# Two interleaved layers on one core: four weight halves kept in layer B's buffer, first loads by whole units, x first, and the first step's last projection by halves

## The chip, the cores and the metric

The kernel runs on one core of one Trainium2 chip. The metric is device time in microseconds (us), median of several runs. The profiled execution is one more run; the profile gives its span, from the first to the last instruction, and its own time is 1.7 us longer.

## The reference

Two kinds of layer follow each other twice: A, B, A, B, each with a layer norm before and a residual sum behind it.

```
def _A_ref(x, mem0, Wq, Wk, Wv, Wo, seg_len):      # Dm = 640, 32 heads of 192, 8 memory rows, segments of 32
    for s in range(n_seg):                         # S = 2048, so 64 segments
        h = concatenate([mem, xs], axis=1)         # 8 + 32 rows
        q, k, v = h @ Wq, h @ Wk, h @ Wv
        p = softmax(where(mask, q @ k.T * scale, -1e9))
        o = (p @ v) @ Wo
        mem = o[:, :M]                             # goes into the next segment
        outs.append(o[:, M:])

def _B_ref(x, wqkv, wo):                           # 32 heads of 20, window of 8 keys, two apart
    q, k, v = x @ wqkv
    return softmax(q . k[pos - 2 * (0..7)]) . v @ wo

x = x + A(layernorm(x));  x = x + B(layernorm(x))
x = x + A(layernorm(x));  x = x + B(layernorm(x))
```

Layer A is sequential over its 64 segments, since each segment's first 8 output rows are the memory of the next. Both A layers use the same weights, and so do both B layers. All tensors are bf16. Layer A's four weights have 640 x 6144 elements each, 31.5 MB together, more than the core's on-chip memory holds.

## The kernel before

**Steps and lanes.** `run` calls `step(t)` for t from 0 to 66. Lane 0 holds the first A, B pair at segment t, lane 1 the second pair at segment t - 2, so a two-lane step multiplies 2 x 40 = 80 columns by each weight. Steps 0 and 1 have lane 0 alone, steps 64 and 65 lane 1 alone (40 columns), and step 66 is `b_alone`, a last block of layer B. Layer B in step t works on the block that layer A finished in step t - 1; so step 0 has no layer B, and step 1 is the first that needs its weights.

**A step.** The heads of layer A are taken four at a time, in 8 quads. For each quad `i`: keys (`a_k`), queries (`a_q`), the product with the values of the quad before (`a_pv`), values (`a_v`, in one-lane steps by `a_v_rows` for all quads but 2 and 3), and scores (`a_s`). From quad 5 on the output projection of quad `i - 5` (`a_o`) comes between; the last ones follow behind quad 7, and `a_o(7)` is the last, after which `mem_out` copies the memory into the next step's input `hT`. Layer B is woven in: its queries and keys (`b_q`, `b_k`) behind the values of quad 1, its values (`b_v`) at quad 2, its output (`b_wo`) at quad 6.

**Weights.** Each of the 32 units (kind k, q, v or o, quad 0 to 7) is cut into two halves of 128 rows x 1920 elements (480 KB, 3,840 bytes in each row). Of the 64 halves 41 stay on chip from the first step on (`resident_halves`); 23 are streamed again in every step through a ring of 4 buffers (`w_ring`). The first four of the streamed ones are, in order of use, one half each of k0, v0, k1 and v1; the next are both halves of k2, one of v2, one of k3, one of q3. `self.loads` is the list of all loads in order: the 64 halves of the first step, the 23 of the second with the four parts of layer B's weights put between them, then 23 for each later step. `prefetch` takes from its front as long as the first entry is resident, a part of layer B, or a ring buffer is free; `used` gives a ring buffer back. First loads take a half in one transfer, later ones in two pieces of 960 elements (1,920 bytes in each row).

**Queues.** All these loads are issued by SP, in the order of the list, and each waits on SP until its buffer is free and until the transfer that used the same one of eight DMA semaphores before it has landed. The loads of x for later steps go by ScalarE's queue at quad 1 and take their turn in the same round of semaphores. The order of work on each engine is written out by hand (`manual_schedule`).

**Layer B's buffers** `wqkv_sb` (three parts of 5 x 640 elements in each partition) and `wo_sb` (one such part) are filled once, in step 1, and stay empty before that.

**The beginning.** `build_consts` clears the constants and buffers on VectorE, the two input buffers `xin` among them. `prologue` issues the load of x (which waits for that clearing), then that of the memory `m0T`, then the weights; the scheduler places the instructions of this part. In step 0 `warm(16)` puts 16 matmuls without use ahead of each of the last output projections.

Of the kernel before, what the change touches and what calls it, by code (L numbers as in the profile page):

```python
# [19 lines left out]
NC = 5  # L20
# [58 lines left out]
class Kernel:  # L79
    def __init__(self, ctx, tc, A_x, A_mem0, A_Wq, A_Wk, A_Wv, A_Wo, B_wqkv, B_wo, out):  # L80
# [33 lines left out]
    def build_consts(self):  # L114
# [20 lines left out]

        self.hT = pers("hT", [P, NC * NT + 88], 1)[0]
# [5 lines left out]
        self.xin = pers("xin", [P, 2, NC, SEG], 2)  # L142
# [8 lines left out]
        self.wqkv = cp.tile([P, 3, NC, D], BF16, name="wqkv_sb")  # L151
        self.wo = cp.tile([P, NC, D], BF16, name="wo_sb")

    def load_b_weights(self, part):

        w = self.wqkv[:, part] if part < 3 else self.wo[:]
# [53 lines left out]
    def prefetch(self):  # L210

        while self.loads and (self.loads[0] in self.resident or self.loads[0][0] == "b" or self.ring_free):
            key = self.loads.pop(0)
            if key[0] == "b":
                self.load_b_weights(key[1])
                continue
            if key in self.resident:
                t_ = self.wres.tile([P, HALF], BF16, name="w_%s%d%d" % key)
            else:
                t_ = self.wring.tile([P, HALF], BF16, name="w_ring")  # L220
                self.ring_free -= 1
            kind, i, h = key
            piece = HALF if self.n_loaded < N_HALVES else PIECE
            self.n_loaded += 1
            for c0 in range(0, HALF, piece):
                self.nc.sync.dma_start(out=t_[:, c0:c0 + piece], in_=self.wsrc[kind][i, h, :, c0:c0 + piece])
            self.units[key] = t_[:].rearrange("p (a b) -> p a b", a=3 if kind == "o" else NC)

    def used(self, kind, i, halves=(0, 1)):

        for h in halves:
            if (kind, i, h) not in self.resident:
                del self.units[kind, i, h]
                self.ring_free += 1
        self.prefetch()
# [136 lines left out]
    def a_o(self, i, part=slice(None), done=True):  # L372
# [5 lines left out]
        order = [(m, c) for m in (0, 2, 3, 5, 1, 4) for c in range(NC)]  # L378
        if i == NQUAD - 1:
            order = [(m, c) for m in (0, 2) for c in range(3)] + [(m, c) for c in range(3) for m in (3, 5, 1, 4)] + [(m, c) for c in range(3, NC) for m in (0, 2, 3, 5, 1, 4)]  # L380
        for m, c in order[part]:
            acc, k = self.acc_of(c)
            nc.tensor.matmul(self.cols(acc[:, k]), lhsT=w[m // 3][:, m % 3, P * c:P * (c + 1)], rhs=self.cols(ot[:, m]),  # L383
                             start=(i == 0 and m == 0 and k == 0), stop=(i == NQUAD - 1 and m == 4), skip_group_check=True)
# [255 lines left out]
    def prologue(self):  # L640
        nc = self.nc
        self.x1, self.ots, self.qxs, self.ebs = {}, {}, {}, {}
        self.x_load(0)
# [132 lines left out]
    def step(self, t):  # L776
# [75 lines left out]
        if t == 0:  # L852
            self.warm(16)
        if nt < T:
            self.ln1_apply(nt)
        self.a_o(7)
# [36 lines left out]
def _lay_out(name, a):  # L893
# [44 lines left out]
```

## Time and profile before

| | |
|---|---|
| runs, median | 3140.94 us (3138.48, 3140.94, 3144.32) |
| profiled execution | 3137.52 us |
| its span | 3135.8 us |
| TensorE busy, matmuls | 3079.3 us, 98% of the span, 83,424 matmuls |
| VectorE, ScalarE, GpSimd busy | 76%, 59%, 18% |
| mean granted clock of TensorE | 0.991 |
| moved by DMA | 786.99 MB, mean 251 GB/s |
| loads of ring buffers, 240 KB each | some 3.8 to 4.1 us from issue to landing |

In a row of a timeline stand the start, the length, the engine, the line, the operation with its operands, the count, and in brackets the idle time before it with what ended it. In the sums over stretches of time each engine's busy time is followed by its count of instructions, and at the end stand the granted clock, the share in which the 16 DMA engines were busy (it can pass 1, as packets overlap) and the rate in GB/s. "issue" is time in which an engine waited for nothing that the profile shows. Of a group of matmuls the length includes the last one's way through the array, about 0.2 us.

### The profile page before, as it was taken

Reading aid. Unit: us, or ns where it says so; the run is one execution under the profiler, and the core shown is the slowest. Engines: PE = TensorE matmul, PEld = TensorE weight load, DVE = VectorE, ACT = ScalarE, POOL = GpSimd, SP = SyncE. Lnnn points to the kernel's source line nnn. Section 1 sums busy time; section 2 is a strip of 40 time slices with the busy share of each in tenths; the row PEclk is TensorE's granted clock in tenths of the full one; section 3 lists DMA queues with packets and bytes.
Section 4 is the critical chain, followed back from the end, with each engine's and each line's share of the span. In section 5 each row is a group of like instructions: output and inputs, shape, how many; then the busy total and the mean of one; then the engine's idle time right before and its main releaser. Section 6 shows DMA issues by size and latency. Waiting matters only on the chain.

```text
span 3135.8 us, 187153 instructions
## 1 busy us (share of the span) xinstructions
PE 3079.3 (98%) x83424; PEld 3031.1 (97%) x83424; DVE 2369.9 (76%) x6012; ACT 1849.2 (59%) x5616; POOL 551.5 (18%) x1025
## 2 busy tenths in 40 slices
PE   6899999999999999999999999999999999999998
PEld 4899999999999999999999999999999999999997
DVE  3677777777777777777777777777777777777775
ACT  2456656656656656656656656656655655655654
POOL 2111111111111111111111111111111111121121
PEclk7999999999999999999999999999999999999999
DMA  9888877777878778887878878877777777877776
GB/s 387 302 249 245 250 243 247 246 245 243 248 246 247 246 246 248 248 247 246 249 244 250 249 246 248 250 241 247 249 245 248 249 242 249 249 246 248 249 250 212
DMA packets 455706, 786.99 MB, mean 251 GB/s; under 512 B 58864, under 2 KB 445680, under 8 KB 454896
## 3 DMA queue, kind: packets, MB, share of 16 engines
q1 hardware_dynamic: 441216, 769.80, 77.8%
q8 instruction: 652, 10.68, 1.4%
q10 hardware_dynamic: 13680, 5.21, 0.7%
q14 instruction: 158, 1.29, 0.1%
HBM read 772.19 MB, written 2.62 MB: 247 GB/s over the span
## 4 chain that ended last, share of the span: by engine, by line
PE 96%; DMA 3%; issue 1%; DVE 0%; ACT 0%; SPq 0%; ACTq 0%
PE ps_acc L383 18%; PE ps_k L266 18%; PE ps_q L266 18%; PE ps_v L266 17%; PE ps_vt L320 5%; PE ps_o L353 5%; PE ps_s L332 2%; PE ps_s L333 2%; PE ps_bs L549 2%; PE ps_bk L497 2%; PE ps_by L608 1%; PE ps_bv L497 1%; PE ps_bq L497 1%; DMA w_q<-in_A_Wq_dram 1%; PE ps_vr L300 1%; PE ps_bo L575 1%
## 5 line engine op out<-in xcount | busy, mean ns | idle before, releaser
L357 ACT ACTIVATE R<-ps_o 64x160 f32<-64x160 f32 (+1 forms) x2112 | 622.1, 295 | 339.3 <-PE ps_o L353 121.3
L266 PEld LDWEIGHTS <-w_ring 128*128 128x128 bf16 x16530 | 679.8, 100 | 23.2 <-issue 7.3
L266 PE MATMUL ps_q<-hT,w_q 128*128 128x80 bf16 (+1 forms) x12870 | 541.8, 201 | 4.0 <-DMA w_q<-in_A_Wq_dram 3.4
L534 POOL TENSOR_TENSOR QX<-QB,hmask 128x448 bf16<-128x448 bf16 (+2 forms) x325 | 304.7, 946 | 1346.1 <-ACT QB L512 1028.2
L266 PEld LDWEIGHTS <-w_q 128*128 128x128 bf16 x12870 | 494.2, 100 | 5.3 <-DMA w_q<-in_A_Wq_dram 4.4
L383 PE MATMUL ps_acc<-OT,w_o 128*128 128x80 bf16 (+1 forms) x9900 | 458.9, 201 | 4.2 <-issue 2.2
L278 ACT CAST KF<-ps_k 128x320 bf16<-128x320 f32 (+1 forms) x528 | 218.9, 415 | 411.8 <-PE ps_k L266 401.5
L311 DVE CAST vT<-ps_v 128x480 bf16<-128x480 f32 (+1 forms) x504 | 329.1, 653 | 163.7 <-PE ps_v L266 145.9
L285 DVE CAST QT<-ps_q 128x480 bf16<-128x480 f32 (+1 forms) x528 | 337.4, 639 | 120.9 <-PE ps_q L266 117.9
L266 PE MATMUL ps_v<-hT,w_v 128*128 128x80 bf16 (+1 forms) x9480 | 423.1, 201 | 2.0 <-DMA w_v<-in_A_Wv_dram 1.1
L383 PEld LDWEIGHTS <-w_o 128*128 128x128 bf16 x9900 | 393.2, 100 | 5.0 <-issue 2.3
L266 PE MATMUL ps_k<-hT,w_ring 128*128 128x80 bf16 (+1 forms) x7920 | 374.3, 201 | 6.6 <-DMA w_ring<-in_A_Wk_dram 2.5
L266 PE MATMUL ps_k<-hT,w_k 128*128 128x80 bf16 (+1 forms) x7920 | 374.0, 201 | 4.3 <-issue 3.3
L266 PEld LDWEIGHTS <-w_v 128*128 128x128 bf16 x9480 | 371.4, 100 | 1.5 <-DMA w_v<-in_A_Wv_dram 1.4
L335 ACT ACTIVATE E<-ps_s 80x320 bf16<-80x320 f32 (+1 forms) x528 | 221.1, 419 | 240.0 <-PE ps_s L333 240.0
L367 DVE TENSOR_TENSOR OT<-ps_o,R 128x320 bf16<-128x320 f32 (+1 forms) x528 | 253.9, 481 | 138.4 <-ACT R L359 117.2
L266 PEld LDWEIGHTS <-w_k 128*128 128x128 bf16 x7920 | 321.8, 100 | 5.0 <-issue 3.5
L322 DVE COPY Vt<-ps_vt 80x768 bf16<-80x768 bf16 x504 | 279.1, 554 | 58.3 <-PE ps_vt L320 46.6
L383 PE MATMUL ps_acc<-OT,w_ring 128*128 128x80 bf16 (+1 forms) x5940 | 307.8, 201 | 2.2 <-DMA w_ring<-in_A_Wo_dram 2.2
L266 PE MATMUL ps_v<-hT,w_ring 128*128 128x80 bf16 (+1 forms) x5640 | 264.6, 201 | 0.7 <-DMA w_ring<-in_A_Wv_dram 0.6
L341 DVE TENSOR_TENSOR E<-E,maskA 80x320 bf16<-80x320 bf16 (+1 forms) x528 | 206.3, 391 | 65.3 <-ACT E L335 54.9
L320 PE MATMUL ps_vt<-ident,vT 128*128 128x128 bf16 x3024 | 253.4, 220 | 0.9 <-DVE On L590 0.9
(146 smaller groups left out, 4914.3 us busy)
## 6 DMA issues: line engine op xcount, KB each, us to landing
w_ring<-in_A_Wk_dram SPq DMA_DIRECT2D x1040, 240.0 KB, 3.8
w_ring<-in_A_Wv_dram SPq DMA_DIRECT2D x780, 240.0 KB, 4.1
w_ring<-in_A_Wo_dram SPq DMA_DIRECT2D x780, 240.0 KB, 3.8
w_ring<-in_A_Wq_dram SPq DMA_DIRECT2D x390, 240.0 KB, 3.9
w_q<-in_A_Wq_dram SPq DMA_DIRECT2D x13, 480.0 KB, 8.8
w_v<-in_A_Wv_dram SPq DMA_DIRECT2D x10, 480.0 KB, 9.6
w_o<-in_A_Wo_dram SPq DMA_DIRECT2D x10, 480.0 KB, 9.6
w_ring<-in_A_Wk_dram SPq DMA_DIRECT2D x8, 480.0 KB, 7.7
```

Of the source, the lines that this page charges most:

```text
L266: nc.tensor.matmul(ps[:, NT * n + self.c0:NT * n + self.c1], lhsT=w[n // 3][:, c, P * (n % 3):P * (n % 3 + 1)], rhs=hT[:, NT * c + self.c0 ...
L278: nc.scalar.copy(out=kf, in_=pv[:, :, 0:3:2, :])
L285: self.nc.vector.tensor_copy(out=self.cols(qt[:]), in_=self.cols(ps[:, 0:6 * NT].rearrange("p (a n) -> p a n", a=6)))
L311: nc.vector.tensor_copy(out=self.cols(self.vT[:, 0:6 * NT].rearrange("p (a n) -> p a n", a=6)), in_=self.cols(ps[:, 0:6 * NT].rearrange("p ...
L320: nc.tensor.transpose(out=ps[:, n, :], in_=self.vT[:, NT * n:NT * n + P], identity=self.ident[:])
L322: nc.vector.tensor_copy(out=vt[0:NT, :].rearrange("p (a b c) -> p a b c", a=2, b=2)[:, :, :, 0:DH], in_=ps[0:NT].rearrange("p (a b) c -> p ...
L335: nc.scalar.activation(out=self.cols(e[0:NT]), in_=self.cols(sv[0:NT]), func=ACT.Exp, scale=float(DH) ** -0.5)
L341: nc.vector.tensor_tensor(out=self.cols(e[0:NT]), in0=self.cols(e[0:NT]), in1=self.cols(self.maskA[0:NT, :]).unsqueeze(1).to_broadcast([NT ...
L357: nc.scalar.activation(out=self.cols(r[r0:r0 + 64, :, j]), in_=self.cols(src), func=ACT.Ln)
L367: nc.vector.tensor_tensor(out=oc[:, :, 0:3:2], in0=ov[:, :, 0:4:3], in1=r, op=ALU.mult)
L383: nc.tensor.matmul(self.cols(acc[:, k]), lhsT=w[m // 3][:, m % 3, P * c:P * (c + 1)], rhs=self.cols(ot[:, m]), start=(i == 0 and m == 0 an ...
L534: self.nc.gpsimd.tensor_tensor(out=qx[:, 0:nh, self.on], in0=self.qb[:, c, self.on].unsqueeze(1).to_broadcast([P, nh, n]), in1=self.hmask[ ...
```

## The change

It has four parts.

- **Four halves kept.** `wqkv_sb` and `wo_sb` become one tile, `wb_sb`, of the same size. In the first step the first four streamed halves are loaded into it, at elements 0, 6400, 8320 and 10240 of each partition, and stay for their second use in step 1. The second step's list holds streamed halves 4 to 7, then the four parts of layer B's weights together, then the other streamed halves. A part of layer B's weights is loaded when the halves that lie in its place have been used twice; `prefetch` returns until then, so what follows it in the list waits too. From step 2 on all 23 halves go through the ring as before.
- **Whole units by rows of 7,680 bytes.** The two halves of a unit now lie side by side in memory. Where both are resident, the first step loads them with one transfer into one tile, except the last output projection's. This makes 15 transfers out of 30. Streamed halves are still loaded in pieces of 1,920 bytes, now from rows 7,680 bytes apart.
- **x first.** The load of x is issued in `build_consts`, ahead of the clearing; the half of `xin` that it fills is not cleared any more. m0 and the weights follow.
- **The last projection by halves.** In step 0 `a_o(7)` runs as 15 matmuls on its first half of the weights and 15 on its second, with 8 warming matmuls ahead of the first and 16 ahead of the second. The second 15 finish the columns of the first accumulator before those of the other.

```diff
-        second = list(streamed)
-        for at, part in ((4, 0), (5, 1), (8, 2), (18, 3)):
-            second.insert(at, ("b", part, 0))
+        self.kept = streamed[:4]
+        self.kept_uses = {u: 0 for u in self.kept}
+        second = streamed[4:8] + [("b", part, 0) for part in range(4)] + streamed[8:]
...
+        self.xin = pers("xin", [P, 2, NC, SEG], 2, zero=False)
+        self.x_load(0)
...
-        self.xin = pers("xin", [P, 2, NC, SEG], 2)
+        nc.vector.memset(self.xin[0][:, 1], 0.0)
+        nc.vector.memset(self.xin[1][:], 0.0)
...
+        self.wb = cp.tile([P, 4 * NC * D], BF16, name="wb_sb")
+        wb = self.wb[:].rearrange("p (a c n) -> p a c n", a=4, c=NC)
+        self.wqkv, self.wo = wb[:, 0:3], wb[:, 3]
+        self.kept_at = dict(zip(self.kept, (0, 2 * NC * D, 2 * NC * D + HALF, 2 * NC * D + 2 * HALF)))
+
+    def under(self, part):
+
+        lo, hi = part * NC * D, (part + 1) * NC * D
+        return [u for u in self.kept if self.kept_at[u] < hi and self.kept_at[u] + HALF > lo]
...
+            if kind == "b":
+                if any(self.kept_uses[u] < 2 for u in self.under(i)):
+                    return
+                self.loads.pop(0)
+                self.load_b_weights(i)
                 continue
+            if first and key in self.kept:
+                at = self.kept_at[key]
+                t_ = self.wb[:, at:at + HALF]
+            elif key in self.resident:
+                n += h == 0 and (kind, i, 1) in self.resident and (kind, i) != ("o", NQUAD - 1)
+                t_ = self.wres.tile([P, n * HALF], BF16, name="w_%s%d%d" % key)
...
+            piece = n * HALF if first else PIECE
+            self.n_loaded += n
+            for c0 in range(0, n * HALF, piece):
+                self.nc.sync.dma_start(out=t_[:, c0:c0 + piece], in_=self.wsrc[kind][i, :, h * HALF + c0:h * HALF + c0 + piece])
...
+        if t == 0:
+            order = [(m, c) for m in (0, 2, 1) for c in range(NC)] + [(m, c) for cs in ((0, 1, 2), (3, 4)) for m in (3, 5, 4) for c in cs]
+            self.warm(8)
+            self.a_o(7, slice(0, 3 * NC), False, order)
+            self.warm(16)
+            self.a_o(7, slice(3 * NC, None), True, order)
+        else:
+            self.a_o(7)
...
-        return a.reshape(NC, P, NQUAD, 2, QE // 2).transpose(2, 3, 1, 0, 4).reshape(NQUAD, 2, P, HALF)
+        return a.reshape(NC, P, NQUAD, 2, QE // 2).transpose(2, 1, 3, 0, 4).reshape(NQUAD, P, 2 * HALF)
...
-        return a.reshape(NQUAD, 2, 3, P, D).transpose(0, 1, 3, 2, 4).reshape(NQUAD, 2, P, HALF)
+        return a.reshape(NQUAD, 2, 3, P, D).transpose(0, 3, 1, 2, 4).reshape(NQUAD, P, 2 * HALF)
```

More of the change, by code (lines that the diff above doesn't have):

```diff
@@ L220, in prefetch @@
                 t_ = self.wring.tile([P, HALF], BF16, name="w_ring")
                 self.ring_free -= 1
[L222 to L227, printed above, removed]
+            else:
+                return
@@ L231, in used @@
         for h in halves:
-            if (kind, i, h) not in self.resident:
-                del self.units[kind, i, h]
-                self.ring_free += 1
+            u = (kind, i, h)
+            if u in self.resident:
+                continue
+            if self.kept_uses.get(u, 2) < 2:
+                self.kept_uses[u] += 1
+                if self.kept_uses[u] == 2:
+                    del self.units[u]
+                continue
+            del self.units[u]
+            self.ring_free += 1
@@ L370, in a_norm, with a_o @@
         self.ots[i] = ot
-    def a_o(self, i, part=slice(None), done=True):
+    def a_o(self, i, part=slice(None), done=True, order=None):
         nc = self.nc
@@ L377, in a_o @@
         w = [self.units["o", i, h] for h in range(2)]
-        order = [(m, c) for m in (0, 2, 3, 5, 1, 4) for c in range(NC)]
-        if i == NQUAD - 1:
+        if order is None and i == NQUAD - 1:
             order = [(m, c) for m in (0, 2) for c in range(3)] + [(m, c) for c in range(3) for m in (3, 5, 1, 4)] + [(m, c) for c in range(3, NC) for m in (0, 2, 3, 5, 1, 4)]
+        if order is None:
+            order = [(m, c) for m in (0, 2, 3, 5, 1, 4) for c in range(NC)]
         for m, c in order[part]:
```

25 lines of the change are left out of this document (11 added, 14 removed).

## The prediction

> **What bounds the kernel now.** I read the page first, then the waits of TensorE between 132 and 3040 us, the sums over stretches of time, the chain that ended last, and TensorE's timeline in the two steps that the change touches. The header of the page, one stretch of the middle, and the first of TensorE's six groups of waits there (five are "issue", one DVE, none a DMA; 6.0 us together):
>
> ```profile
> span 3135.8 us, 187153 instructions
> 180.00:3000.00 2820.00, 2813.73 (x76522) 2794.35 (x76519) 2188.34 (x5477) 1708.75 (x5114) 494.26 (x840) 1.00 0.80 247
> PE ps_k L266 <- issue: 1.8, 6, 0.4
> ```
>
> TensorE is busy for 2813.73 of 2820 us. The two-lane steps are bound by it, and nothing in the change takes work from it there. What can be won lies before 132 us. There the bound is another one (stretches: PE, PEld, DVE, ACT, POOL busy, clock, DMA share, GB/s; then the chain, start and length):
>
> ```profile
> 18.00:23.00 5.00, 4.19 (x106) 3.33 (x102) 2.74 (x9) 2.26 (x10) 3.58 (x21) 1.00 1.00 367
> 40.00:60.00 20.00, 12.90 (x226) 9.43 (x226) 5.15 (x15) 5.64 (x23) 0.00 (x0) 0.67 1.03 406
> 84.00:88.00 4.00, 3.95 (x93) 3.10 (x90) 2.95 (x10) 1.10 (x4) 0.00 (x0) 1.00 1.06 386
> 37.44 9.60 DMA w_q<-in_A_Wq_dram
> 47.05 10.15 DMA w_q<-in_A_Wq_dram
> ...
> 86.69 6.73 DMA wqkv_sb<-in_B_wqkv_dram
> ```
>
> The first step waits for 64 halves of 0.49 MB (31.5 MB) that come at 406 GB/s with the engines' share at 1.03: the DMA engines are full, and step 0 ends when the last half lands. Step 1 begins in the same regime and leaves it by degrees. TensorE's timeline there (start, length, what, idle before it and its cause):
>
> ```profile
> 83.69 0.78 PE L383 MATMUL ps_acc<-OT,w_o 128*128 128x40 bf16 x24 [0.89 <-DMA w_o<-in_A_Wo_dram]
> 84.44 0.23 PE L266 MATMUL ps_k<-hT,w_ring 128*128 128x40 bf16 x3
> ...
> 88.99 0.91 PE L266 MATMUL ps_q<-hT,w_q 128*128 128x40 bf16 x30
> ...
> 91.56 0.78 PE L497 MATMUL ps_bq<-h2T,wqkv_sb 128*128 128x32 bf16 x25
> ...
> 93.47 0.71 PE L497 MATMUL ps_bk<-h2T,wqkv_sb 128*128 128x32 bf16 x22 [0.87 <-DMA wqkv_sb<-in_B_wqkv_dram]
> ...
> 94.23 0.23 PE L266 MATMUL ps_k<-hT,w_ring 128*128 128x40 bf16 x3
> 94.69 0.85 PE L266 MATMUL ps_k<-hT,w_ring 128*128 128x40 bf16 x15 [0.23 <-DMA w_ring<-in_A_Wk_dram]
> 95.92 0.28 PE L266 MATMUL ps_k<-hT,w_ring 128*128 128x40 bf16 x3 [0.38 <-DMA w_ring<-in_A_Wk_dram]
> 96.33 1.17 PE L266 MATMUL ps_q<-hT,w_q 128*128 128x40 bf16 x30
> 97.97 0.77 PE L497 MATMUL ps_bv<-h2T,wqkv_sb 128*128 128x32 bf16 x22 [0.40 <-DMA wqkv_sb<-in_B_wqkv_dram]
> 103.64 0.47 PE L266 MATMUL ps_q<-hT,w_ring 128*128 128x40 bf16 x12 [0.54 <-DMA w_ring<-in_A_Wq_dram]
> 107.96 0.37 PE L353 MATMUL ps_o<-E,Vt 80*128 80x40 bf16 x8 [0.29 <-DVE Vt L322]
> 117.76 0.25 PE L266 MATMUL ps_k<-hT,w_k 128*128 128x40 bf16 x4 [2.26 <-issue]
> 127.02 0.54 PE L383 MATMUL ps_acc<-OT,w_ring 128*128 128x40 bf16 x15 [0.97 <-DMA w_ring<-in_A_Wo_dram]
> 130.94 1.14 PE L383 MATMUL ps_acc<-OT,w_o 128*128 128x40 bf16 x30
> ```
>
> Step 1 runs from 84.44 to 132.08, 47.6 us. The kernel has a second step of the same shape, the last one (one lane of 40 columns, 32 columns of layer B), with DMA to spare. Its rows:
>
> ```profile
> 3080.76 0.23 PE L266 MATMUL ps_k<-hT,w_ring 128*128 128x40 bf16 x3
> ...
> 3088.47 0.78 PE L497 MATMUL ps_bk<-h2T,wqkv_sb 128*128 128x32 bf16 x25
> 3089.29 0.91 PE L266 MATMUL ps_k<-hT,w_ring 128*128 128x40 bf16 x30
> ...
> 3098.16 0.57 PE L266 MATMUL ps_k<-hT,w_ring 128*128 128x40 bf16 x15 [1.12 <-issue]
> ...
> 3120.15 0.95 PE L383 MATMUL ps_acc<-OT,w_o 128*128 128x40 bf16 x30
> ```
>
> From 3080.76 to 3121.10: 40.3 us. So step 1 has 7.3 us that its work does not need. Part of it is clock (the last stretches give TensorE's busy time, clock, DMA share and GB/s alone):
>
> ```profile
> 92.31:95.73 3.42, 1.96 (x53) 1.00 1.03 383
> 95.73:99.14 3.41, 2.83 (x79) 0.50 0.96 350
> 99.14:102.55 3.41, 3.34 (x83) 0.50 0.64 192
> ```
>
> **The change, part by part.** *Rows of 7,680 bytes.* Fifteen whole units (30 halves, 14.75 MB) come in one transfer each; SP issues 15 instructions fewer, off the path. Rows of 1,920 bytes moved at 386 GB/s and rows of 3,840 at 406. If the cost per row is constant, its share halves with each doubling: per byte 1/386 - 1/406 is 0.128 ns per KB, half of it goes again, and 1/406 becomes 1/417. 14.75 MB then take 35.4 us for 36.3: -0.9 us. Ends: 0 (longer rows bring nothing; a loss is excluded by the order of the two rows) and, as no later row shows the effect, double, -1.8.
>
> The Trainium skill, "DMA: Bandwidth & Descriptors", Where 436 GB/s comes from, puts the ports' ceiling at 435 GB/s. No stretch here reaches it; at that rate the same bytes would be an estimated 2.4 us cheaper, and the sum 1.5 us lower.
>
> *x first.*
>
> ```profile
> 0.81 0.38 SPq L644 DMA_DIRECT2D m0T<-in_A_mem_dram  x1
> 1.24 0.42 SPq L226 DMA_DIRECT2D w_ring<-in_A_Wk_dram  x1
> ...
> 3.31 0.33 SPq L620 DMA_DIRECT2D xin<-in_A_x_dram  x1
> ```
>
> x now precedes m0 and the weights and waits for no memset, so the first weight is issued one instruction (0.33 to 0.43 us) later: +0.4 at a start that the full DMA engines do not make good. Ends: 0 and +0.5. The layer norm of x comes some 2.5 us sooner (the row at 3.31 against 0.81), which I cost at nothing: from 21 us on TensorE waits for weights. Without that cover it would be -2.5.
>
> *Four halves in layer B's buffer.* In step 0 the ring's four slots are then free for the next four, and SP waits less for TensorE. The stretch 18 to 23 us moved 367 GB/s; at 406 that would be 0.5 us. Its share is 1.00, so not all of it was starvation: -0.2, ends 0 and -0.5.
>
> *Last projection by halves.* After the last landing 15 matmuls remain and not 24, at 0.78 / 24 = 0.03 us: -0.2. The eight added warming matmuls (and the moved sixteen) stand before the last landing, where 0.89 us of idle time covers them; without it, they cost 0.4.
>
> Step 0: -0.9 + 0.4 - 0.2 - 0.2 = **-0.9 us**, ends -2.5 and +0.3.
>
> *Step 1.* Four halves (1.97 MB) less are loaded in it. Up to layer B's keys this brings nothing: before, k0, v0, k1, v1 and two parts of layer B's weights (3.6 MB) landed between the last half of step 0 and 93.42; after, k2 (two halves), v2, k3 and the same two parts do, the same 3.6 MB. The first part waits for k0's second use, about 1 us into the step, when 1.97 MB are still queued ahead of it (5 us at 386), so the wait is covered. The stall before the keys stays: k(2) began 9.79 us into the step, 8.53 in the last step, so 1.3 of the 7.3 remain. After it k2, v2 and k3 lie there already, and parts 2 and 3 were queued at about 4 and 7 us of the step. On SP the later ring halves queue behind part 3, which waits for v(1); they need the slot that k(2) frees, two projections later, so they lose nothing. The waits 0.23, 0.38, 0.40 and 0.54 go, and so should the 0.97. What is late next is the ring's refill. SP also waited once for the load of x, which stands in the shared round of DMA semaphores:
>
> ```profile
> SPq L226 <- DMA xin<-in_A_x_dram: 3.5, 1, 3.5
> w_ring<-in_A_Wk_dram SPq DMA_DIRECT2D x1040, 240.0 KB, 3.8
> ```
>
> In the new order this falls on the second half of v4, which is wanted some 5 us later; a landing takes 3.8.
>
> The half clock from 95.73 to 102.55 followed a stretch with TensorE busy for 1.96 of 3.42 us. A group of 30 matmuls took 1.17 cold and 0.91 warm, so 6 us of work lost some 1.5. With one wait of about 1.3 us in place of four it need not fall. The 2.26 us of "issue" I keep (1.1 more than the last step's 1.12), and the 0.29 for Vt. So 7.3 - 1.3 - 1.1 - 0.3 = **-4.6 us**. Check from below: waits of 2.5 and clock of 1.5 are 4.0. Ends: -1.5 (three waits only) and -6.0 (the gap shrinks too, and the stall stays).
>
> Sum -5.5 us. The profiled execution took 3137.52 us (3135.8 of span and 1.7 around it), 3.4 below the median of 3140.94 of the runs. Execution 3132.0, median **3135.4**.
>
> **The rivals.**
> (a) The clock falls again, through the stall before the keys. The Trainium skill, "TensorE: Matmul & The Clock Gate", Part 1, lets it fall after an idle window of about 3.4 us; by that no wait here would do it. The trace differs: it fell after 57% busy. A stall of 1.3 in 3.4 us leaves 62%, if it lies in one window. Then +1.5: 3136.9.
> (b) More goes: rows at the lower end (-0.9 more), the dip whole (-0.3) and the gap of 2.26 as in the last step (-1.1): -7.8, 3133.1. Such gaps came at different places in each one-lane step, which speaks for luck.
> (c) The waits only move: with four slots the refill of the ring is late after k4, as at 127.02, and step 1 keeps all but 1.5. Sum -2.4: 3138.5. For it: 0.97 us were lost there once nothing older was in the way. Against it: the last step asks for the same halves at the same pace, and its gap at 3098.16 is "issue", no transfer.
> (d) Slower: the streamed pieces of all later steps now come from rows 7,680 bytes apart and not 3,840. If that slows them, TensorE waits in each of 62 two-lane steps. The tightest place is the four halves of Wo, issued together:
>
> ```profile
> 2038.22 6.91 SPq L226 DMA_DIRECT2D w_ring<-in_A_Wo_dram  x8
> ...
> 2051.72 0.52 PE L383 MATMUL ps_acc<-OT,w_ring 128*128 128x80 bf16 x10
> ```
>
> The last piece goes at about 2044.7 (the end of the group, less its own 0.4), lands after 3.8 us, and its half is used from 2051.72, 3.2 us later. So landing must nearly double before it decides. It would take 0.19 us in each step to be slower by 0.2% (5.5 + 6.3 = 11.8 over 62): above 3147.
>
> **How the numbers follow.** What a measurement of this kernel can tell is about 0.2%, 6.3 us: 3134.7 to 3147.2. Forecast 0.40, (a) 0.16, (b) 0.27, (c) 0.09, (d) 0.08. The forecast stands 0.8 us from the bound and is uncertain by 2 to 3, so 0.4 of it counts as faster, of (b) 0.85, of (a) 0.1: 0.16 + 0.23 + 0.02 = 0.41. Slower is (d), 0.08; the rest 0.51 is no change. The range leaves (d) out, reaches below (b) by the ends of its terms and the runs' own spread of 3 us, and above (c) by the same: 3128.5 to 3142.5.
>
> **What would show it.** Right: k(0) of step 1 about 1 us sooner than 84.44; the stretch 40 to 60 above 410 GB/s; a wait before the keys of about a microsecond and none for k2, layer B's values and q3; step 1 about 43 us; the two-lane steps as before. Wrong: half clock after the keys (a), waits for ring halves after k4 (c), any DMA among TensorE's waits between 132 and 3040 us (d), or no higher rate in step 0.

## The result and the profile after

The changed kernel takes 3132.88 us (median of 11 runs, 3126.11 to 3136.32); before takes 3139.47 us beside it (11 runs, 3135.96 to 3149.31). The ratio is 0.9976, with a 95% interval of 0.9967 to 0.9984: faster by 0.24%. The profiled execution of the changed kernel took 3134.59 us, 2.9 less than that of before.

TensorE's timeline of the changed kernel from the end of step 0 to the start of step 2, where 82.69 and 127.57 are the first key matmuls of steps 1 and 2:

```profile
80.83 0.54 PE L415 MATMUL ps_acc<-OT,w_o 128*128 128x40 bf16 x15 [0.22 <-DMA w_o<-in_A_Wo_dram]
...
82.03 0.55 PE L415 MATMUL ps_acc<-OT,w_o 128*128 128x40 bf16 x15
82.69 0.23 PE L297 MATMUL ps_k<-hT,wb_sb 128*128 128x40 bf16 x3
...
91.77 0.24 PE L529 MATMUL ps_bk<-h2T,wb_sb 128*128 128x32 bf16 x3 [1.39 <-DMA wb_sb<-in_B_wqkv_dram]
...
92.59 0.75 PE L529 MATMUL ps_bk<-h2T,wb_sb 128*128 128x32 bf16 x22 [0.58 <-DMA wb_sb<-in_B_wqkv_dram]
...
93.44 1.17 PE L297 MATMUL ps_k<-hT,w_ring 128*128 128x40 bf16 x30
94.44 1.17 PE L297 MATMUL ps_q<-hT,w_q 128*128 128x40 bf16 x30
...
102.46 0.47 PE L297 MATMUL ps_k<-hT,w_ring 128*128 128x40 bf16 x12 [0.34 <-DMA w_ring<-in_A_Wk_dram]
...
116.51 0.86 PE L297 MATMUL ps_k<-hT,w_k 128*128 128x40 bf16 x28 [0.29 <-issue]
...
122.17 0.68 PE L415 MATMUL ps_acc<-OT,w_o 128*128 128x40 bf16 x21 [0.91 <-issue]
...
126.99 0.61 PE L415 MATMUL ps_acc<-OT,w_o 128*128 128x40 bf16 x18 [1.35 <-issue]
127.57 0.27 PE L297 MATMUL ps_k<-hT,w_ring 128*128 128x80 bf16 x3
```

Step 0 ends 1.75 us sooner (84.44 before). Step 1 takes 44.88 us where it took 47.5 (two-lane keys began at 131.94 before, so 2.6 less). Five of the DMA waits of before are gone; one is left, before layer B's keys (1.39 + 0.58), and a new small one at k4 (0.34). What else is left is "issue".

The sums over stretches, changed kernel:

```profile
2.00:4.00 2.00, 0.00 (x0) 0.00 (x0) 1.97 (x6) 0.09 (x1) 1.69 (x10) 1.00 0.65 117
...
18.00:23.00 5.00, 3.07 (x42) 2.16 (x42) 1.39 (x4) 1.13 (x5) 3.76 (x24) 0.82 1.01 408
40.00:60.00 20.00, 14.16 (x226) 9.30 (x224) 5.33 (x16) 5.65 (x23) 0.00 (x0) 0.76 1.03 410
...
89.40:92.80 3.40, 1.43 (x39) 1.13 (x37) 1.32 (x5) 0.83 (x3) 1.33 (x3) 1.00 1.01 392
92.80:96.20 3.40, 3.40 (x115) 3.40 (x112) 0.65 (x2) 1.20 (x5) 0.00 (x0) 0.51 0.70 236
...
180.00:3000.00 2820.00, 2813.47 (x76486) 2793.32 (x76483) 2186.85 (x5471) 1708.30 (x5113) 496.87 (x842) 1.00 0.79 247
```

Step 0 moves 410 GB/s in the stretch 40 to 60 for 406, and 408 from 18 to 23 for 367. After the stall before the keys the clock falls to one half for 3.4 us (before: 6.8). In the two-lane steps TensorE is idle for 6.53 of 2820 us, before for 6.27: no change there.

The page's header, and its row for the loads of instructions, which a later section needs:

```profile
span 3132.9 us, 187143 instructions
...
q8 instruction: 652, 10.68, 1.4%
```

Step 2 starts 4.37 us sooner and the span is only 2.9 us shorter. From step 2's start on the changed kernel takes 3005.3 us and before 3003.9. TensorE's idle time there is the same (18.4 and 18.7 us), so the difference lies in what counts as busy. In the other profiles that stream weights the same part takes 2999 to 3007 us, though its work is the same: that spread is larger than the whole change. So the experiments are read by their stages, and the medians only bound them.

### The profile page after: what moved, and what is told of

It is laid out like the page before. It is cut to its first block, busy times and chain, and to the rows that moved or that the text cites. A ratio compares the mean times of both kernels' runs of the same rounds, so it can differ in the third digit from the quotient of the medians.

```text
span 3132.9 us, 187143 instructions
## 1 busy us (share of the span) xinstructions
PE 3079.6 (98%) x83432; PEld 3030.0 (97%) x83432; DVE 2369.5 (76%) x6012; ACT 1848.9 (59%) x5616; POOL 552.8 (18%) x1025
## 3 DMA queue, kind: packets, MB, share of 16 engines
q8 instruction: 652, 10.68, 1.4%
q14 instruction: 158, 1.29, 0.1%
## 4 chain that ended last, share of the span: by engine, by line
PE 96%; DMA 3%; issue 1%; DVE 0%; ACT 0%; SPq 0%; ACTq 0%
PE ps_acc L415 18%; PE ps_k L297 18%; PE ps_q L297 17%; PE ps_v L297 17%; PE ps_vt L351 5%; PE ps_o L384 5%; PE ps_s L363 2%; PE ps_s L364 2%; PE ps_bs L581 2%; PE ps_bk L529 2%; PE ps_by L640 2%; PE ps_bv L529 2%; PE ps_bq L529 1%; PE ps_bo L607 1%; PE ps_vr L331 1%; DMA w_ring<-in_A_Wv_dram 1%
## 5 line engine op out<-in xcount | busy, mean ns | idle before, releaser
L297 PEld LDWEIGHTS <-w_ring 128*128 128x128 bf16 x16470 | 676.8, 100 | 17.1 <-issue 3.4
L415 PEld LDWEIGHTS <-w_ring 128*128 128x128 bf16 x5940 | 248.9, 100 | 5.1 <-issue 2.4
## 6 DMA issues: line engine op xcount, KB each, us to landing
w_ring<-in_A_Wk_dram SPq DMA_DIRECT2D x6, 480.0 KB, 10.4
```

What stands on the lines that cost most here:

```text
L297: nc.tensor.matmul(ps[:, NT * n + self.c0:NT * n + self.c1], lhsT=w[n // 3][:, c, P * (n % 3):P * (n % 3 + 1)], rhs=hT[:, NT * c + self.c0 ...
```

## The experiments

All times in us. "Idle" is 2820 less TensorE's busy time in the stretch 180 to 3000. The kernels were measured in four sets, each with before beside it (its medians there are 3137.39 to 3140.04), so kernels are compared by the ratio rather than by the median.

| kernel | step 1 starts | step 1 takes | idle | median (runs) | ratio to before, 95% |
|---|---|---|---|---|---|
| before | 84.44 | 47.50 | 6.3 | 3139.47 (11) | 1 |
| changed | 82.69 | 44.88 | 6.5 | 3132.88 (11) | 0.9976 (0.9967 to 0.9984) |
| e8_again, the changed kernel again | 83.00 | 41.62 | 4.6 | 3129.88 (5) | 0.9972 (0.9960 to 0.9984) |
| e1_halves | 87.06 | 41.48 | 3.7 | 3131.11 (6) | 0.9967 (0.9952 to 0.9982) |
| e11_halves_x1 | 83.70 | 43.16 | 3.5 | 3132.05 (10) | 0.9984 (0.9975 to 0.9993) |
| e2_x_late | 83.17 | 42.17 | 5.2 | 3130.28 (5) | 0.9968 (0.9955 to 0.9981) |
| e6_a7_whole | 82.98 | 42.99 | 4.0 | 3132.15 (6) | 0.9973 (0.9962 to 0.9985) |
| e3_none_kept | 83.03 | 48.10 | 3.3 | 3135.01 (10) | 0.9986 (0.9977 to 0.9996) |
| e5_pitch_only | 83.74 | 48.06 | 4.6 | 3136.46 (10) | 0.9992 (0.9982 to 1.0001) |
| e4_keys_first | 83.56 | 42.74 | 5.8 | 3131.95 (11) | 0.9975 (0.9966 to 0.9984) |
| e10_output_later | 82.73 | 43.87 | 5.3 | 3131.43 (11) | 0.9980 (0.9971 to 0.9988) |
| e12_both | 83.17 | 42.49 | 5.7 | 3131.06 (11) | 0.9979 (0.9970 to 0.9988) |
| e7_warm_keys | 82.80 | 44.63 | 3.3 | 3132.00 (9) | 0.9980 (0.9970 to 0.9990) |
| e9_no_stream | 82.74 | 42.44 | 0.0 | 3114.51 (2) | 0.9927 (0.9908 to 0.9945) |

**The changed kernel once more (e8_again).** No edit.

> The changed kernel itself once more, for a second profile. Theory: what the loads set comes back within 0.5 us (step 1 begins at 82.2 to 83.2, stall before the keys 1.5 to 2.2 us), while the gaps called issue come at other places and with other sums (10 to 14 us over the span); so a difference of 1 to 2 us between single profiles in the two-lane steps means nothing. Rival: the gaps stand at the same places as in the first profile, and are a property of the kernel.

TensorE's timeline around the stall, and the start of step 2:

```profile
92.51 0.71 PE L529 MATMUL ps_bk<-h2T,wb_sb 128*128 128x32 bf16 x22 [1.51 <-DMA wb_sb<-in_B_wqkv_dram]
...
124.62 0.27 PE L297 MATMUL ps_k<-hT,w_ring 128*128 128x80 bf16 x3
```

The same program takes 41.62 us for step 1 where its first profile took 44.88. The stall is there (1.51), the clock does not fall after it, and the issue gaps sum to 1.4 us and not 2.7. So some 3 us of step 1 are luck, more than any one term of the prediction but the largest. (The gaps have fixed places, as the last section shows; which of them appear, and how long they are, changes.)

**Nothing kept (e3_none_kept).** The rest of the change stays.

```diff
-        self.kept = streamed[:4]
+        self.kept = []
-        second = streamed[4:8] + [("b", part, 0) for part in range(4)] + streamed[8:]
+        second = list(streamed)
+        for at, part in ((4, 0), (5, 1), (8, 2), (18, 3)):
+            second.insert(at, ("b", part, 0))
```

> The changed kernel with nothing kept in layer B's buffer and the second step's loads in the order of before; the other three parts stay. Theory: step 1 is as long as before (47 to 48 us, the changed kernel has 45.0), with waits for k2, layer B's values and q3 back and half clock for 3.4 to 6.8 us; step 0 loses the free ring again: 18 to 23 us at 370 to 395 GB/s for 408, and step 1 begins 0.3 to 0.8 us later than 82.69. Total 3 to 3.5 us above the changed kernel. Rival (step 1 was shorter by the luck of the clock, not by the fewer bytes): step 1 stays within 0.7 us of 45.0.

TensorE's waits in its step 1, grouped (sum, times, longest), then a stretch of its step 0:

```profile
PE ps_k L299 <- DMA w_ring<-in_A_Wk_dram: 2.5, 6, 0.8
PE ps_bk L531 <- DMA wb_sb<-in_B_wqkv_dram: 1.4, 2, 0.8
PE ps_k L299 <- issue: 1.0, 2, 0.5
PE ps_acc L417 <- issue: 0.8, 1, 0.8
PE ps_bv L531 <- DMA wb_sb<-in_B_wqkv_dram: 0.6, 1, 0.6
PE ps_q L299 <- DMA w_ring<-in_A_Wq_dram: 0.2, 1, 0.2
```

```profile
18.00:23.00 5.00, 2.96 (x30) 1.88 (x30) 1.02 (x3) 1.26 (x6) 3.69 (x22) 0.80 1.02 409
```

The waits for ring halves and layer B's values are back, and step 1 takes 48.1 us. Three profiles without kept halves (before, this, the next) give 47.5 to 48.1, mean 47.9; the seven with them and with the changed kernel's order of loads (changed, e8, e1, e11, e2, e6, e7) give 41.5 to 44.9, mean 43.0. The two groups do not overlap: keeping the halves, with the order of loads that it allows, is worth 4.9 us by the stages. The totals agree only within their width: the ratios of e3 and of the changed kernel are 0.0010 apart, 3.1 us, and their intervals overlap. The stretch 18 to 23 moves 409 GB/s though nothing is kept, so the freed ring is not what filled the dip of before.

**Before with the new layout alone (e5_pitch_only).** Transfers and order as before; only the rows in memory lie 7,680 bytes apart.

```diff
-                self.nc.sync.dma_start(out=t_[:, c0:c0 + piece], in_=self.wsrc[kind][i, h, :, c0:c0 + piece])
+                self.nc.sync.dma_start(out=t_[:, c0:c0 + piece], in_=self.wsrc[kind][i, :, h * HALF + c0:h * HALF + c0 + piece])
```

> The kernel before with nothing but the new layout in memory: every transfer as before, its rows now 7,680 bytes apart and not 3,840. Theory: no difference from the kernel before in any stage: step 0 ends at 84.4, step 1 takes 47.6, the two-lane steps 46.72, landings 3.7 to 3.8 us. Rival (the pitch slows or speeds the streamed pieces): landings move by over 0.3 us; only if they pass 7 us do waits for DMA appear in the two-lane steps.

Two stretches of its step 0, then the start of its step 1:

```profile
18.00:23.00 5.00, 3.56 (x75) 2.62 (x71) 2.37 (x7) 2.25 (x11) 3.69 (x21) 1.00 1.02 403
40.00:60.00 20.00, 12.54 (x213) 8.68 (x210) 5.09 (x15) 5.65 (x23) 0.00 (x0) 0.76 1.03 405
```

```profile
83.74 0.26 PE L266 MATMUL ps_k<-hT,w_ring 128*128 128x40 bf16 x3
```

Idle time in the two-lane steps is 4.6 us, and the ratio 0.9992 includes no change: rival (d) did not occur, and the layout by itself does nothing that can be measured. (Its sign, a wait for ring halves in the two-lane steps, is absent in before, e5 and both profiles of the changed kernel; e2, e3, e4, e10 and e12 have one or two such waits, 0.2 to 0.7 us together in each.) This kernel has before's order of loads, and the dip is missing here too (403), with step 1 0.7 us sooner. So the dip of before's profile does not belong to its order of work, and a part of the 1.75 us that step 0 seemed to gain is not the change's.

**First loads by halves (e1_halves, e11_halves_x1).** e1 takes the merging of whole units away; e11 does the same and loads x(1) at the very start, by SP.

```diff
-                n += h == 0 and (kind, i, 1) in self.resident and (kind, i) != ("o", NQUAD - 1)
```
```diff
+        self.nc.sync.dma_start(out=self.xin[1][:, 0], in_=self.x[1])
...
-                if nt < self.n_seg:
+                if 1 < nt < self.n_seg:
                     self.x_load(nt)
```

> The changed kernel with every half loaded by its own transfer again (rows of 3,840 bytes, out of rows 7,680 apart). Theory of the prediction (a row has a constant cost): the stretch 40 to 60 us falls from 410 to about 406 GB/s, the first key matmul of step 1 comes 0.9 us later than the changed kernel's 82.69, so at 83.6; total 0.9 us above the changed kernel. Rival (longer rows bring nothing, step 0 was shortened by the free ring alone): 410 GB/s stays, 82.7, no difference. Steps from 3 on 46.72 us either way.

e1 began step 1 at 87.06, far later than rows could explain. SP's timeline of e1, SP's group of waits for x, and three stretches of step 0:

```profile
24.66 0.33 SPq L248 DMA_DIRECT2D w_ring<-in_A_Wq_dram  x1
31.40 0.81 SPq L248 DMA_DIRECT2D w_v<-in_A_Wv_dram  x2
```

```profile
SPq L248 <- DMA xin<-in_A_x_dram: 6.4, 1, 6.4
```

```profile
30.00:31.00 1.00, 0.74 (x18) 0.75 (x19) 0.00 (x0) 0.03 (x1) 0.00 (x0) 0.50 0.26 88
31.00:32.00 1.00, 0.97 (x18) 0.70 (x16) 0.39 (x1) 0.60 (x3) 0.47 (x1) 0.50 0.12 50
...
30.00:40.00 10.00, 5.29 (x113) 4.44 (x114) 2.22 (x7) 2.19 (x9) 3.70 (x10) 0.50 0.78 294
```

SP issues nothing between 24.66 and 31.40, because the next weight's turn in the round of DMA semaphores comes behind the load of x(1), issued by ScalarE at 24.18 among full queues. By 30 us the queued halves had run out and the DMA engines stood nearly empty; the stretch of 10 us moves 294 GB/s, at 404 that is 2.7 us lost. (The totals can't show it: this very execution took 3130.42, a little under e1's median.) At the end of the step the 16 warming matmuls, at half clock, took 1.24 us for 0.73 and cost a little more (see e6).

e11 was made to take that wait away.

> All halves in transfers of their own, as in the first run of this study, with the second step's x loaded at the start by SP, so that no load of ScalarE's queue stands in the round of DMA semaphores during step 0. Theory: the hole of 30 to 33 us there (294 GB/s between 30 and 40) came from SP waiting for that x, which had to wait among the weights; without it the stretch 30 to 40 has 404 to 408 GB/s and step 1 begins at 83.5 to 84.2. Rival: the hole has another cause or was a chance of that one profile; then 30 to 40 us shows a hole again, or the run says nothing.

SP now issues the next weight at 24.79, right behind the one at 24.41. The stretch:

```profile
30.00:40.00 10.00, 7.25 (x155) 6.23 (x156) 2.78 (x8) 2.81 (x12) 0.00 (x0) 0.51 1.03 405
```

The hole is absent here, and step 1 starts at 83.70. Ten profiles with merged units start step 1 at 82.69 to 83.56, mean 82.99; this one, at 404 to 407 GB/s for some 410, 0.71 us later. That is not the rows alone: with x(1) at the start e11 issues its first weight 0.47 us later (2.18 for 1.71). Two pairs share the start of the weights, and are compared by the landing of the last one, which the clock does not move. e12, with x(1) at the start and merged units, has it at 82.46, e11 at 82.99: 0.53. e2 (below), with x late as in e5, has it at 81.97, e5 at 82.84: 0.87. So longer rows are worth 0.5 to 0.9 us, by two pairs of single profiles. The changed kernel has the same gap on SP:

```profile
24.66 0.33 SPq L249 DMA_DIRECT2D w_v<-in_A_Wv_dram  x1
28.24 1.66 SPq L249 DMA_DIRECT2D w_ring<-in_A_Wk_dram  x2
...
83.56 3.55 SPq L170 DMA_DIRECT2D wb_sb<-in_B_wqkv_dram  x6
89.63 0.33 SPq L170 DMA_DIRECT2D wb_sb<-in_B_wo_dram  x1
```

It passes without a hole (409 GB/s from 20 to 40). That the larger units are the reason is not shown, and the record speaks against it: before and e5 load halves too, and move 403 and 407 GB/s from 30 to 40. What sets e1 apart is when ScalarE lets x(1) go: at 24.18, for 21.31 in before, 20.83 in e5 and 22.44 in the changed kernel, while it lands 5.7 to 7.2 us later in each. Two kernels with merged units that issue it almost as late, e4 at 23.68 and e9 at 23.59, have 400 and 403 GB/s there, a small dip. So the lateness of x(1) goes with the hole in these profiles; whether the size of the units has a part in it was not tried by itself.

**x late (e2_x_late).** x again after the clearing, weights first.

```diff
-        self.xin = pers("xin", [P, 2, NC, SEG], 2, zero=False)
-        self.x_load(0)
...
+        self.xin = pers("xin", [P, 2, NC, SEG], 2)
...
+        self.x_load(0)
         nc.sync.dma_start(out=self.m0T[:], in_=self.mem0)
```

> The changed kernel with the load of x where it was before, behind the clearing of its buffer and among the weights. Theory of the prediction: the first weight goes 0.4 us sooner, TensorE starts some 3 us later (12.4 for 9.6), and step 1 begins 0.4 us sooner than 82.69, at 82.3. Rival (x first pays: TensorE, 3 us late, releases the ring too late and the transfers starve for a while): a stretch between 10 and 40 us below 405 GB/s, and step 1 begins 0.3 to 1 us later, at 83.0 to 83.7.

Two stretches of e2:

```profile
2.00:4.00 2.00, 0.00 (x0) 0.00 (x0) 1.97 (x6) 0.08 (x1) 1.69 (x10) 1.00 0.79 195
20.00:30.00 10.00, 6.60 (x169) 5.42 (x166) 4.25 (x13) 3.84 (x17) 3.95 (x17) 0.92 1.02 399
```

The head start is there: 195 GB/s from 2 to 4 us where the changed kernel moves 117, 0.16 MB or 0.4 us at 406. 20 to 30 moves 399 for 409, which gives 0.25 of it back. Both signs of the rival are met, a stretch below 405 and a start at 83.17, but neither tells: e4 and e9, with x first, have 400 and 403 from 30 to 40, and the late start comes from the clock, which was at half when the last weight had landed (see e6). The landing itself, 81.97, is the earliest of the kernels with merged units by 0.01, and 0.25 sooner than the mean of the eight with x first and x(1) in its old place (81.98 to 82.85). So the 0.4 us of the theory is neither shown nor excluded.

**The last projection whole (e6_a7_whole).**

```diff
+        if t == 0:
+            self.warm(16)
...
-        if t == 0:
+        if False:
```

> The changed kernel with the last output projection of step 0 as before (16 warming matmuls, then 30 in the old order). Theory of the prediction: 24 matmuls instead of 15 stand behind the last landing, so step 1 begins 0.2 us later (82.9 for 82.69). Rival: the 24 warming matmuls of the split stand in the way when the clock is at half, so that the old order is as fast or faster (82.3 to 82.7).

Its last group of step 0:

```profile
82.23 0.78 PE L415 MATMUL ps_acc<-OT,w_o 128*128 128x40 bf16 x24 [0.89 <-DMA w_o<-in_A_Wo_dram]
```

Step 1 starts at 82.98, between the two profiles of the changed kernel (82.69 and 83.00). Counted from the landing of the last weight it can be told apart: 82.19 in e6 and 83.65 in before, 0.79 us ahead of step 1 in both; 81.98 in the changed kernel, 0.71 ahead, and 0.71 or 0.72 in the eight other profiles with the split and full clock there. So the split gains 0.08 us and not 0.2. In e6 step 1 follows the 24 matmuls directly. In the changed kernel TensorE is through its 15 at about 82.5, and then waits for the memory's first copy into `hT`, which in e6 is done by the time the 24 are. The copies by VectorE in e6 and in the changed kernel:

```profile
82.74 0.48 DVE L433 CAST hT<-ps_acc 128x24 bf16<-128x24 f32 x2 [5.61 <-PE ps_acc L415]
82.46 0.33 DVE L433 CAST hT<-ps_acc 128x24 bf16<-128x24 f32 x2 [5.38 <-PE ps_acc L415]
```

So the copy, which starts 0.55 us behind the landing in e6, starts only 0.07 sooner with the split (0.48), and step 1 can begin no sooner than it ends. At half clock the split loses: 1.17 and 1.20 us pass from the landing to step 1 in e1 and e2, for 0.90 in e5, which has no split. There the warming matmuls were in the way, as the rival had it.

**The order of layer B's weights (e4_keys_first, e10_output_later, e12_both).** The keys' part, under which no kept half lies, goes first in the second step's list, in place of behind four ring halves and the queries' part. The diff is that of e4; e10 has 15 for both 12, which puts the output's part three halves later. e12 is e10 with e11's early x(1).

```diff
-        second = streamed[4:8] + [("b", part, 0) for part in range(4)] + streamed[8:]
+        b = [("b", part, 0) for part in range(4)]
+        second = [b[1]] + streamed[4:6] + [b[0], b[2]] + streamed[6:12] + [b[3]] + streamed[12:]
```

> The changed kernel with another order of step 1's loads: layer B's key part (nothing lies under it) first, then both halves of k2, the query part, the value part, four further streamed halves (v2, k3, q3, k4 and both next), the output part behind the second k4 and v4 halves. Theory: the changed kernel's stall before the keys (1.4 + 0.6 us) comes from the 3.6 MB queued up to the key part; now 0.8 MB are up to the keys and 2.6 MB up to the queries, which land 6.2 us into the step and are wanted at 6.9. So no stall there, the clock does not fall behind it (0.9 us), and the hole of 93 to 97 us is filled: step 1 from 44.9 to 41.5 to 42.5 us, total 2.5 to 3.5 us below the changed kernel. Rival: the waits move to the value part or to k3 and q3, and step 1 stays above 44.

The stall before the keys is gone in e4, and a later one has come:

```profile
106.53 0.47 PE L298 MATMUL ps_k<-hT,w_ring 128*128 128x40 bf16 x12 [1.31 <-DMA w_ring<-in_A_Wk_dram]
```

SP issues the output's part at 98.10 ahead of k5, which is then late by 1.31.

> The order of loads with layer B's keys first, as in the run with that order, but with the output part only behind the first half of Wo, where the kernel before had it. Theory: that order removed the stall before the keys and brought one of 1.3 us for k5, behind the output part; with this part later no wait for DMA is left in step 1 but some under 0.3 us, step 1 takes 40.5 to 43 us by the gaps called issue, total 1 to 2 us below the changed kernel, which a measurement can hardly tell. Rival: the ring of four is late at k5 or Wo anyway, with waits of about 1 us.

> The changed kernel with the order of loads of the run before last (keys first, output part behind the first half of Wo) and the second step's x loaded at the start. Theory: step 1 begins at 82.5 to 83.2, its stall before the keys is gone, step 1 takes 40.5 to 43; total 1 to 2.5 us below the changed kernel. Rival: no difference, since what is won at the keys is lost to the ring.

In e10 and e12 no DMA wait is left in step 1. All of e12's waits there, grouped:

```profile
PE ps_k L299 <- issue: 1.7, 3, 1.2
PE ps_acc L417 <- issue: 0.8, 1, 0.8
PE ps_v L299 <- issue: 0.7, 1, 0.7
```

Step 1 still takes 42.5 us in e12 and 43.9 in e10, about the mean of 43.0 with the stall. The issue gaps alone sum to 3.1 in e12 and 3.2 in e10, whose clock also fell for 3.4 us behind a gap of 1.38. Taking the last DMA wait away gained nothing that these runs can show; the medians, 3131.06 to 3131.95, lie among those of the changed kernel.

**Warming before the keys (e7_warm_keys).** 24 warming matmuls behind layer B's queries.

```diff
             self.b_q(b)
+            if b == 0:
+                self.warm(24)
             self.b_k(b)
```

> The changed kernel with 24 useless matmuls (about 1.1 us) between layer B's queries and keys in step 1, where it waits for 2.0 us. Theory: the stall for the key part stays at the same time, but TensorE is busy in it, so the clock does not fall to half behind it; the 60 matmuls of k2 and q2 take 1.5 us for 2.0, and step 1 is 0.5 to 0.9 us shorter (44.0 to 44.4 for 44.9). Rival: the clock falls all the same, or the fall cost nothing since other engines bound those quads: 44.9.

```profile
92.36 0.28 PE L719 MATMUL ps_warm<-ident 128*128 128x80 bf16 x3 [1.12 <-issue]
```

The wait for the keys' part is gone, but 1.12 us of issue now stand inside the warming itself. The clock holds behind the keys, and falls for 3.4 us from 98.6 on, after an issue gap of 1.33 us at 97.16. Step 1 takes 44.63 us, the ratio is 0.998: nothing is won.

**No streamed weights (e9_no_stream).**

```diff
-        self.loads = [u for u, _ in order] + second + streamed * (self.n_seg + LAG - 2)
+        self.loads = [u for u, _ in order] + second + []
...
+        if self.t >= 2:
+            return
...
+                self.units[u] = self.last[j % RING][:].rearrange("p (a b) -> p a b", a=3 if u[0] == "o" else NC)
```

> The changed kernel with no weights streamed from step 2 on: the 23 streamed halves of each later step are read from the four ring buffers as step 1 left them. So the later products are computed with wrong weights, but with the same instructions on TensorE; steps 0 and 1 are unchanged. It measures the gaps called issue. Theory: TensorE's next instructions come by the same DMA engines as the weights, and the weights' packets delay them; with 90% of the traffic gone the sum of the steps 3 to 63 above 61 times 46.72 us falls from 6 to 12 us to under 2, and the span by 5 to 12 us. Rival: the gaps come from TensorE's own pace of instructions; the sum stays at 6 us or more.

The middle of the run:

```profile
180.00:3000.00 2820.00, 2820.00 (x76774) 2802.72 (x76770) 2197.21 (x5491) 1714.15 (x5137) 498.70 (x845) 1.00 0.02 6
```

TensorE is idle for 0.00 of 2820 us, where every kernel that streams is idle for 3.3 to 6.5. TensorE's instructions are the same, and the page has the same 652 packets of instructions; what is gone is 241 of 247 GB/s of traffic and the waits tied to it, none of which shows as a DMA wait in the middle of the changed kernel. From the start of step 3 to that of step 64 the changed kernel takes 12.2 us longer than e9, so a part of the loss lies inside what counts as busy. The whole span is 19.9 us shorter (3113.0 for 3132.9): besides these 12.2 us, 2.4 lie ahead of step 2, 1.0 in it, and 4.3 in steps 64 to 66.

## Why the prediction was right, and where its terms were not

The sum was -5.5 us, made of -0.9 and -4.6. The medians of 11 runs give -6.6 (interval 5.0 to 10.4, from the ratio), and the stages of the experiments some -0.7 and -4.9. 3132.88 lies 2.5 below the predicted 3135.4, and of that 1.5 is the median of before, which came out at 3139.47 and not 3140.94. By the prediction's own bound of 0.2% the result is faster, to which it gave 0.41, less than to no change (0.51). The large term was right in its mechanism; that step 0 came near was partly luck, since its three small terms, each off or not settled, added to nothing.

- *Rows of 7,680 bytes, -0.9*: right in sign, and in size as far as two pairs of single profiles tell (-0.53 and -0.87). The stretch 40 to 60 reaches 410, the value named as the bound and not above it; 36.3 us for the merged half become 35.4 to 35.8, an estimate of 412 to 416 GB/s for a predicted 417. The ceiling of 435 GB/s in the Trainium skill, "DMA: Bandwidth & Descriptors", Where 436 GB/s comes from, was not reached with the longer rows either.
- *x first, +0.4*: the later start of the weights is seen (117 for 195 GB/s); a later end is not settled. The last landing comes 0.25 us sooner with x late than the mean with x first, but lies within 0.01 of the earliest of these, and they spread over 0.9.
- *Freed ring, -0.2*: wrong. e3 keeps nothing and e5 has the old order, and both move 403 to 409 GB/s in the stretch where before's profile moved 367. The dip was taken for a property of before; it was one of that execution, some 0.7 us by e5's start of step 1 (0.8 by its last landing).
- *Last projection, -0.2*: -0.08 at full clock. The term counted the matmuls behind the landing and left out the copy into `hT`, which comes between them and step 1. The 0.89 us of cover held at full clock (the warming ends at 81.95, the weight lands at 81.98), and did not at half clock.
- *Step 0 together, -0.9*: -0.75 by e5's start of step 1 against the mean of the ten, of which 0.1 is e5's half clock at the end; the profiles' own difference of 1.75 holds the dip.
- *Kept halves, -4.6*: right. 47.9 against 43.0 over ten profiles is -4.9, and the predicted length of "about 43 us" is that mean. The changed kernel's first profile alone, 44.88, would have read as -2.6. The waits for k2, bv and q3 went, as named.
- *The stall stays, 1.3*: right in its cause, small in size. It took 1.97 and 1.51 in the two profiles. That it is the loads queued ahead of the keys' part is shown by e4, where that part comes first and the stall is gone. The first part was issued 0.9 us into the step and the fourth 6.9, as said.
- *The issue gap*: 2.26 was kept, 2.7 and 1.4 us of such gaps were found in two profiles, none of it at the old place. The place is a fixed one (last section), but what stands there is not: behind 1754 or 1755 matmuls before has 2.26, e5 1.29, e10 1.38, e12 1.16, both profiles of the changed kernel nothing.
- *Rival (a), the clock*: occurred in one of the two profiles, and for 3.4 us. The work from the first score behind the keys to the values of quad 2 takes 3.31 us there (93.18 to 96.49) and 2.66 in e8 (93.07 to 95.73), so the fall cost about 0.65 us, not 1.5. The stretch ahead of the fall was busy for 1.43 of 3.40 us; e8, with no fall, for 1.81:

```profile
89.60:93.00 3.40, 1.81 (x51) 1.49 (x49) 1.42 (x5) 0.92 (x4) 1.33 (x3) 1.00 1.03 396
```

  That is less than the 57% at which before's clock fell. In before itself TensorE is busy for 54% of the stretch 116.20 to 119.62, and no fall follows. So no single share decides. The falls in step 1 last 3.4 us or twice that. The Trainium skill, "TensorE: Matmul & The Clock Gate", Part 1, has a window of 3413 ns that runs freely, so that the point of change depends on where in it the first matmul lands; the lengths agree with it, and so does that the same program falls in one execution and not in another. Its condition, an idle window, does not agree: eleven profiles have a fall in step 1, and TensorE was busy for 42 to 75% of the 3.41 us ahead of it.
- *Rival (b), more goes*: by the total this came nearest (3133.1), though as a difference to before -6.6 lies as near to -5.5 as to -7.8. But its reasons were the dip, which was no part of the change, and rows at their lower end, which did not happen.
- *Rival (c), the waits move to the ring*: 0.34 us at k4 in one profile, 0 in the other; of the kernels with the same order e6 has 0.38 there, the others none.
- *Rival (d)*: excluded by e5 as a loss in every step; the idle time in the two-lane steps is 6.5 us in the changed kernel and 4.6 in e5, for 6.3 in before. In the changed kernel all of it is "issue" again:

```profile
PE ps_k L297 <- issue: 2.7, 6, 0.8
```

  (the first of the changed kernel's six groups of TensorE's waits from 180 us on; none is a DMA).

## What to carry to other kernels

Where a filling phase is bound by DMA, buffers that stand empty until later can hold weights for their second use: here four halves kept in them took five waits and 4.9 us out of the next step, with no cost that these runs show. Before a dip or a gap in one profile is priced as something that a change can win, look for it in a second profile of the same kernel: here 3 us of a step came and went without any edit. Time the end of a stage from the event that releases it, here the last landing: that told 0.08 us apart where the starts of step 1 spread over 0.9. And a small load in the queue of another engine can hold the large ones, if both take turns in one round of semaphores, as in e1: it is safer ahead of the flood or well before its turn comes.

## What was not expected of the hardware

**Issue gaps: late blocks of instructions, under traffic.** TensorE's idle time in the two-lane steps, in the changed kernel all of it time in which it waits for nothing in the trace, is 3.3 to 6.5 us in 13 profiles, and 0.00 in e9, where DMA moves 6 GB/s in place of 247. So the streaming brings them; e9 takes away the traffic and the waits tied to it at once. The gaps look scattered, but they come back at the same instruction. The same gap in e8, e4, e10 and e12:

```profile
97.00 0.41 PE L297 MATMUL ps_v<-hT,w_ring 128*128 128x40 bf16 x10 [0.61 <-issue]
95.86 0.41 PE L298 MATMUL ps_v<-hT,w_ring 128*128 128x40 bf16 x10 [0.64 <-issue]
95.86 0.41 PE L298 MATMUL ps_v<-hT,w_ring 128*128 128x40 bf16 x10 [1.48 <-issue]
95.48 0.41 PE L299 MATMUL ps_v<-hT,w_ring 128*128 128x40 bf16 x10 [0.65 <-issue]
```

It stands behind 1371 matmuls from the start; the next ones stand behind 1499, 1627, 1754 or 1755, 1882, 2010, 2138. All 228 issue gaps of the 14 profiles, behind the first few matmuls, lie within 2.4 matmuls of such a ladder with a rung at every 127.95th. e7 shows that the count decides and not the work: its 24 warming matmuls move the work, and its gap at the end of step 1 (1.40 us) again stands behind 2138 matmuls, now ahead of an earlier product. The profile's row of 652 instruction packets and 10.68 MB (16 KB each) fits: the kernel has 83,432 matmuls, each with a weight load, which makes 128 such pairs for each packet. So behind each gap stands the edge of a block of instructions, and a block that comes late under the traffic is the reading that fits place and e9 together; no run moved the blocks alone. The Trainium skill, "Runtime: NRT & Kernel Launch", Instruction fetch mechanics, says that the sequencer fetches its next 16 KiB by a DMA queue of its own and that the cost is mostly hidden; the packets' size agrees, and hidden it is in e9's two-lane steps, while under 247 GB/s some of it is not. Two runs of e9 lay 0.4 us apart and the changed kernel's eleven span 10; two runs are too few to say that the gaps make that spread.

**A load of x that takes 6 us to be let go.** In e1 SP stood for 6.4 us on a load that is small beside a weight half, issued on another engine's queue while the 16 DMA engines were full, and the engines ran dry meanwhile (88 and 50 GB/s). Before and the changed kernel have the same wait with 3.5 and 3.2 us and no hole; there the load was issued 1.7 to 2.9 us sooner.
